# ScalarE's order in the second half of a slot of an expert kernel: rounded rows first, the transposing DMA later

## The chip, the cores and the metric

The kernel runs on one core of a Trainium2 chip. The metric is the time of one execution in device microseconds (us). TensorE (PE) multiplies, VectorE (DVE), ScalarE (ACT) and GpSimd (POOL) work element by element, SyncE (SP) and ScalarE issue DMAs.

## The reference, cut to what matters

An attention with a blocked causal mask is followed by a mixture of eight experts, of which each token uses one. All numbers are float32.

```
q, k, v: (8 batches, 8 heads, 576, 64)
x = softmax(mask(q @ k.T / 8)) @ v          -> 4608 tokens of 512 numbers
expert = argmax(x @ w_gate); gate = softmax weight of that expert
out[token] = gate * (relu(x[token] @ w1[expert]) @ w2[expert])
w1: (8, 512, 1024), w2: (8, 1024, 512)
```

## The kernel before

The first part of the program is the attention with the router. The second part, which begins near 390 us, works on *slots*: 128 tokens that go to the same expert (38 slots in this execution, numbered from 0, each expert's last one filled up). The change touches only this second part. It is written as plain code, in which each engine executes its instructions in the order in which the functions are called, and semaphores (`wait_ge`, `then_inc`) order the engines among each other.

To keep float32 accuracy a factor is split into a rounded part and the rest that the rounding left ("high" and "low"); a product is then made of three rounded products. For one slot `t` the steps are:

- `gather` (POOL) fetches the token rows into `xg`; `rows_in` (PE) transposes them into the PSUM tile `px`.
- `rows_full` (ACT) copies `px` to `xf`, `rows_high` (ACT, line 907) rounds it to `xh`, `rows_pool` (POOL, line 923) makes the rest `xl`.
- `first_half(t, f)` (PE, line 933) makes half `f` of the hidden layer, 512 of its 1024 columns: 8 products that need `xh` and 4 that also need `xl`. It writes the bank `ph` (f = 0) or the bank called `o` in the trace (f = 1). Ahead of half 0 PE's sequencer reads two numbers from memory into registers (lines 965 and 966) and waits for `xh` and `xf`.
- `planes(t, f)` (ACT, line 991) copies that bank into a tile `h` with upper and lower 16 bits apart, `turned(t, f)` (ACT, line 1004) issues a DMA that transposes the tile into `hf` (f = 0) or `turn` (f = 1), `joined(t, f)` (ACT, line 1011) waits for that DMA and puts the 16-bit halves together again, `hidden_high(t, f)` (ACT, line 1020) applies the ReLU and rounds to the high part, `second_relu` (ACT, line 1024) is the ReLU of the unrounded half 1, and `hidden_low(t, f)` (POOL, lines 1051 and 1053) makes the low part. High and low parts both lie in tiles called `low` in the trace.
- `second_pe(t, part)` (PE, line 1083) makes 12 products with half `part`, the last four of which need the low part; `out_act(t)` (ACT, line 1100) scales the result by the gate into `y`, and `out_pool(t)` (POOL, line 1107) writes it out.

DVE meanwhile splits the next expert's weights (lines 1227 and 1233), which SP loads into `raw` (line 1220), as soon as the expert whose place they take is done with.

`period(t)` is one turn of this pipeline. PE's order in it is: half 0 of the first layer of slot t, half 0 of the second layer of slot t-1, the transposes of the rows of slot t+1, half 1 of the first layer of slot t, half 1 of the second layer of slot t-1. ScalarE's order is the order of the calls, and it is what the change alters. `finish` does what is left of the last slot.

Of the kernel before, what the change touches and what calls it, by code (L numbers as in the profile page):

```python
# [792 lines left out]
class Experts:  # L793
# [53 lines left out]
    def run(self):  # L847
# [17 lines left out]
        def gather(t):  # L865
            i = t % 4
            if t < EARLY:
                return
            if t == EARLY:
                pool.wait_ge(sem["ht"], 2)  # L870
                pool.wait_ge(sem["me"], 1)
                pool.wait_ge(sem["st"], 16)
                pool.wait_ge(sem["ga"], 48)
            c = pool.value_load(self.col[t : t + 1, 0:1], min_val=0, max_val=TC - 1)  # L874
            pool.tensor_copy(self.idx[:, t : t + 1], self.stab[:, bass.ds(c, 1)]).then_inc(sem["v1"], 1)  # L875
            pool.wait_ge(sem["v1"], t + 1 - EARLY)
            if t >= 4:
                pool.wait_ge(sem["ya"], t - 3)  # L878
            pool.indirect_dma_start(  # L879
                out=self.xg[i],  # L880
                out_offset=None,
                in_=self.xd[:, :],
                in_offset=bass.IndirectOffsetOnAxis(ap=self.idx[:, t : t + 1], axis=0),
            ).then_inc(sg[i], 16)
# [5 lines left out]
        def rows_in(t):  # L890

            if t >= EARLY:
                pe.wait_ge(sg[t % 4], 16 * gathered(t))
            if t >= 2:
                pe.wait_ge(sem["xa"], 2 * t - 2)
            for k in range(4):
                m = pe.transpose(self.px[:, P * k : P * k + P], self.xg[t % 4][:, P * k : P * k + P], self.ident)
                if t == 1 and k < 2:

                    m.then_inc(sem[("mm1", "mm2")[k]], (3, 1)[k])  # L900
            m.then_inc(sem["xt"], 1)

        def rows_high(t):
            act.wait_ge(sem["xt"], t)
            if t >= 2:
                act.wait_ge(sem["mm1"], 2 * t + 1)
            act.copy(self.xh, self.px).then_inc(sem["xa"], 1)  # L907

        def rows_full(t):
            act.wait_ge(sem["xt"], t)  # L910
            if t >= 2:
                act.wait_ge(sem["xp"], t - 1)
            act.copy(self.xf, self.px).then_inc(sem["xa"], 1)
# [5 lines left out]
        def rows_pool(t):  # L919
            pool.wait_ge(sem["xa"], 2 * t)  # L920
            if t >= 2:
                pool.wait_ge(sem["mm1"], 2 * t + 1)
            pool.tensor_sub(self.xl, self.xf, self.xh).then_inc(sem["xp"], 1)  # L923
# [59 lines left out]
        def planes(t, f):  # L983

            k = 2 * t + f
            act.wait_ge(sem["mm1"], k + 2)
            if k == 4:
                act.wait_ge(sem["ht"], 4)
            elif k >= 7:
                act.wait_ge(sem["hp"], k - 2)  # L990
            act.copy(  # L991
                self.h[k % 3].bitcast(U16).rearrange("p (o c) -> p o c", o=2),
                self.ph[f].bitcast(U16).rearrange("p (c o) -> p o c", o=2),
            ).then_inc(sem["ra"], 1)

        def turned(t, f):

            k = 2 * t + f
            if k == 4:
                act.wait_ge(sem["hp"], 4)  # L1000
            elif k >= 6:
                act.wait_ge(sem["jo"], k - 5)
            act.wait_ge(sem["ra"], k - 1)
            act.dma_start_transpose(
                self.turn[f].bitcast(U16).rearrange("p (k c) -> p k c", c=P), self.h[k % 3].bitcast(U16)
            ).then_inc(st[f], 16)
# [9 lines left out]
        def hidden_high(t, f):  # L1016
            k = 2 * t + f
            act.wait_ge(sem["jo"], k - 3)
            act.wait_ge(sem["mm2"], t)
            act.activation(self.hh[t % 2][:, f], self.h[k % 3], AF.Relu).then_inc(sem["ha"], 2 - f)  # L1020
# [34 lines left out]
        def second_pe(t, part):  # L1055
            e8, off = self.regs[t]
            kinds = ((self.hh, 8192), (self.hl, 8192), (self.hh, 12288))
            if t < 2:
                todo = [(h[t % 2], base, c) for h, base in kinds for c in range(8)]
            else:  # L1060
                todo = [(kinds[i][0][t % 2], kinds[i][1], 4 * f + c) for f in range(2) for i in (0, 2, 1) for c in range(4)]
            if part == 0:
                pe.wait_ge(sem["wh"], e8 + 8 if t >= EARLY else 4)
                if t >= 2:
                    pe.wait_ge(sem["ya"], t - 1)
            if t >= 2:
                pe.wait_ge(sem["ha"], 4 * t + 2 + part)
            elif part == 0:
                pe.wait_ge(sem["ha"], 4 * t + 3)
            for n in range(12 * part, 12 * part + 12):  # L1070
                h, base, c = todo[n]
                if t < 2:
                    if n == 8:
                        pe.wait_ge(sem["hp"], 2 * t + 2)
                    if t == 0 and n >= 16 and c % 2 == 0:
                        pe.wait_ge(sem["wd"], 5 + c // 2)
                    elif n == 16:
                        pe.wait_ge(sem["wd"], e8 + 8)
                elif n == 4:
                    pe.wait_ge(sem["wd"], e8 + 8)  # L1080
                elif n % 12 == 8:
                    pe.wait_ge(sem["hp"], 2 * t + part + 1)
                m = pe.matmul(  # L1083
                    self.py[t % 2],
                    h[:, c // 4, P * (c % 4) : P * (c % 4) + P],
                    wf[:, bass.ds(off + (base + 512 * c), 512)],
                    start=n == 0,
                    stop=n == 23,
                )
            if part == 1:  # L1090
                m.then_inc(sem["mm2"], 1)

        def out_act(t):
            act.wait_ge(sem["mm2"], t + 2)
            if t >= 1:
                act.wait_ge(sy, 16 * t)
            else:

                act.wait_ge(sem["ga"], 48)
            act.activation(self.y, self.py[t % 2], AF.Copy, scale=self.xg[t % 4][:, GATE : GATE + 1]).then_inc(  # L1100
                sem["ya"], 1
            )

        def out_pool(t):
            pool.drain()  # L1105
            pool.wait_ge(sem["ya"], t + 1)
            pool.indirect_dma_start(  # L1107
                out=self.out[:, :],
                out_offset=bass.IndirectOffsetOnAxis(
                    ap=(self.router.first if t < EARLY else self.idx)[:, t : t + 1], axis=0  # L1110
                ),
                in_=self.y,
                in_offset=None,
                bounds_check=self.out.shape[0] - 1,
                oob_is_err=False,
            ).then_inc(sy, 16)
# [21 lines left out]
        def late_half(t):  # L1138
            joined(t, 1)
            hidden_high(t, 1)  # L1140
            second_relu(t)

        def period(t):
            more = t + 1 < NS
            if t == 2:

                for f in range(2):
                    planes(t, f)
                    turned(t, f)
                for f in range(2):  # L1150
                    second_pe(0, f)
                out_act(0)
                out_pool(0)
                gather(4)
                second_pe(1, 0)
                rows_in(3)
                second_pe(1, 1)
                rows_full(3)
                rows_high(3)
                rows_pool(3)  # L1160
                joined(t, 0)
                hidden_high(t, 0)
            else:
                first_half(t, 0)
                planes(t, 0)
                turned(t, 0)
                second_pe(t - 1, 0)
                late_half(t - 1)
                hidden_low(t - 1, 1, pool)
                if more:  # L1170
                    rows_in(t + 1)
                    rows_full(t + 1)
                first_half(t, 1)
                planes(t, 1)
                turned(t, 1)
                if more:
                    rows_high(t + 1)
                    rows_pool(t + 1)
                second_pe(t - 1, 1)
                joined(t, 0)  # L1180
                hidden_high(t, 0)
            out_act(t - 1)
            hidden_low(t, 0, pool)
            out_pool(t - 1)
            if t + 3 < NS:
                gather(t + 3)
# [251 lines left out]
```

## Time and profile before

| | us |
|---|---|
| median of 3 runs (lowest to highest) | 874.76 (873.31 to 879.41) |
| the profiled execution, its own time | 877.96 |
| its span on the core | 876.0 |
| PE busy | 815.2 |
| ACT busy | 597.2 |
| DVE busy | 433.2 |
| POOL busy | 417.7 |

The profiled execution was 3.20 us slower than the median, and 1.96 us of its time lie outside the span. The span falls in two stages: attention and router until some 390 us, the slots after that. In the second stage a period repeats some three dozen times, so a tenth of a microsecond in a period is worth several microseconds in the whole.

### The profile page before, as it was taken

Reading aid. Unit: us, or ns where it says so; the run is one execution under the profiler, and the core shown is the slowest. Engines: PE = TensorE matmul, PEld = TensorE weight load, DVE = VectorE, ACT = ScalarE, POOL = GpSimd, SP = SyncE. Lnnn points to the kernel's source line nnn. Section 1 sums busy time; section 2 is a strip of 40 time slices with the busy share of each in tenths; the row PEclk is TensorE's granted clock in tenths of the full one; section 3 lists DMA queues with packets and bytes.
Section 4 is the critical chain, followed back from the end, with each engine's and each line's share of the span. In section 5 each row is a group of like instructions: output and inputs, shape, how many; then the busy total and the mean of one; then the engine's idle time right before and its main releaser. Section 6 shows DMA issues by size and latency. Waiting matters only on the chain. (4 is left out here: it accounts for less than half of the span.)

```text
span 876.0 us, 16317 instructions
## 1 busy us (share of the span) xinstructions
PE 815.2 (93%) x4982; PEld 614.1 (70%) x4982; DVE 433.2 (49%) x1208; ACT 597.2 (68%) x1254; POOL 417.7 (48%) x428
## 2 busy tenths in 40 slices
PE   5999999999999999998798999999999999999994
PEld 4777767677777777676676777776776777777773
DVE  5778777778787877487017000067367462000000
ACT  6888888888888888444456566655565555656563
POOL 3000223222323422455557656667767666656664
PEclk8999999999999999999999999999999999999997
DMA  5234748363636363528837643468867973434332
GB/s 194 95 116 157 134 134 161 123 151 120 138 125 132 118 133 118 128 60 255 151 91 180 163 97 85 81 173 201 233 174 214 220 187 85 85 73 97 90 79 64
DMA packets 121803, 118.51 MB, mean 135 GB/s; under 512 B 83633, under 2 KB 86961, under 8 KB 121714
## 3 DMA queue, kind: packets, MB, share of 16 engines
q1 hardware_dynamic: 38082, 78.26, 32.1%
q10 hardware_dynamic: 76032, 18.88, 14.0%
q0 software_dynamic: 7600, 20.24, 7.1%
q8 instruction: 49, 0.80, 0.4%
q14 instruction: 40, 0.33, 0.2%
HBM read 77.02 MB, written 21.98 MB: 113 GB/s over the span
## 5 line engine op out<-in xcount | busy, mean ns | idle before, releaser
L1083 PE MATMUL py<-w,low 128*128 (+1 forms) x912 | 232.3, 401 | 14.4 <-POOL low L1053 8.1
L1083 PEld LDWEIGHTS py<-w,low 128*128 128x128 f32 x912 | 171.7, 190 | 62.3 <-POOL low L1053 16.9
L1227 DVE CAST w<-raw 128x1024 fp32r<-128x1024 f32 x60 | 55.6, 967 | 197.9 <-PE o L933 152.6
L247 POOL TENSOR_SCALAR p<-p,rs 128x64 f32<-128x64 f32 x32 | 14.1, 442 | 259.0 <-DVE rs L243 139.8
L1053 POOL TENSOR_TENSOR low<-h,low 128x512 fp32r<-128x512 f32 x72 | 96.9, 1346 | 10.0 <-ACT h L1024 6.7
L933 PE MATMUL ph<-w,xh 128*128 x280 | 73.9, 406 | 22.6 <-ACT xh L907 17.7
L923 POOL TENSOR_TENSOR xl<-xf,xh 128x512 fp32r<-128x512 f32 x38 | 52.8, 1389 | 79.6 <-ACT xh L907 79.5
L1233 DVE TENSOR_TENSOR w<-raw,w 128x1024 fp32r<-128x1024 f32 x60 | 88.8, 1537 | 0.0
L933 PEld LDWEIGHTS ph<-w,xh 128*128 128x128 f32 x280 | 50.8, 189 | 46.1 <-issue 37.7
L1011 ACT COPY h<-turn 128x1024 uint16<-128x1024 uint16 x36 | 42.1, 1169 | 55.6 <-issue 46.1
L933 PE MATMUL o<-w,xh 128*128 x280 | 72.9, 403 | 0.0
L1051 POOL TENSOR_SCALAR h<-h 128x512 f32<-128x512 f32 x36 | 60.9, 1691 | 14.5 <-ACT low L1020 14.4
L1107 POOL DMA_INDIRECT out<-y,idx x35 | 45.7, 1305 | 40.0 <-issue 37.2
L991 ACT COPY h<-ph 128x1024 uint16<-128x1024 uint16 x36 | 36.4, 1012 | 39.5 <-PE ph L933 39.5
L907 ACT CAST xh<-px 128x512 fp32r<-128x512 f32 x38 | 22.3, 586 | 58.5 <-issue 52.5
L991 ACT COPY h<-o 128x1024 uint16<-128x1024 uint16 x36 | 36.4, 1012 | 35.9 <-PE o L933 33.0
L933 PEld LDWEIGHTS o<-w,xh 128*128 128x128 f32 x280 | 50.0, 189 | 8.8
L879 POOL DMA_INDIRECT xg<-xd,idx x38 | 45.4, 1196 | 12.7 <-POOL idx L875 12.7
L234 ACT ACTIVATE pb<-ya,neg 128x320 f32<-128x320 f32 (+2 forms) x93 | 48.5, 532 | 2.5 <-PE pt30x L273 1.8
L234 ACT ACTIVATE pb<-yb,neg 128x320 f32<-128x320 f32 (+2 forms) x93 | 49.4, 546 | 0.0
L731 POOL DMA_INDIRECT tab<-toks,posi x40 | 41.7, 1042 | 15.1 <-issue 14.6
L1020 ACT ACTIVATE low<-h 128x512 fp32r<-128x512 f32 x72 | 45.5, 632 | 4.3 <-issue 0.4
(967 smaller groups left out, 2152.6 us busy)
## 6 DMA issues: line engine op xcount, KB each, us to landing
raw<-w SPq DMA_DIRECT2D x60, 512.0 KB, 5.7
qd<-qT SPq DMA_DIRECT2D x32, 352.0 KB, 3.1
v<-vt SPq DMA_DIRECT2D x32, 352.0 KB, 4.7
kd<-kT SPq DMA_DIRECT2D x32, 288.0 KB, 3.3
xd<-xt SPq DMA_DIRECT2D x7, 1026.0 KB, 12.1
xd<-xg SPq DMA_DIRECT2D x9, 256.5 KB, 6.8
xg<-w SPq DMA_DIRECT2D x8, 256.0 KB, 6.5
xd<-x SPq DMA_DIRECT2D x8, 128.0 KB, 6.6
```

The source lines that it names most:

```text
L234: ins = self.nc.scalar.activation(dst, src, AF.Exp, bias=self.neg[m][:, c : c + 1], scale=1.0, accum_out=self.sums[m][:, c : c + 1])
L879: pool.indirect_dma_start(out=self.xg[i], out_offset=None, in_=self.xd[:, :], in_offset=bass.IndirectOffsetOnAxis(ap=self.idx[:, t : t + 1 ...
L923: pool.tensor_sub(self.xl, self.xf, self.xh).then_inc(sem["xp"], 1)
L933: m = pe.matmul(self.ph[f], x[:, P * k : P * k + P], first_weights(t, k, f, part), start=start and k == 0, stop=stop and k == 3,)
L991: act.copy(self.h[k % 3].bitcast(U16).rearrange("p (o c) -> p o c", o=2), self.ph[f].bitcast(U16).rearrange("p (c o) -> p o c", o=2),).the ...
L1020: act.activation(self.hh[t % 2][:, f], self.h[k % 3], AF.Relu).then_inc(sem["ha"], 2 - f)
L1051: engine.tensor_scalar(hf, hf, 0.0, None, ALU.max).then_inc(sem["rl"], 1)
L1053: engine.tensor_sub(self.hl[t % 2][:, f], hf, self.hh[t % 2][:, f]).then_inc(sem["hp"], 1)
L1083: m = pe.matmul(self.py[t % 2], h[:, c // 4, P * (c % 4) : P * (c % 4) + P], wf[:, bass.ds(off + (base + 512 * c), 512)], start=n == 0, st ...
L1107: pool.indirect_dma_start(out=self.out[:, :], out_offset=bass.IndirectOffsetOnAxis(ap=(self.router.first if t < EARLY else self.idx)[:, t ...
L1227: dve.tensor_copy(hi, raw[m % nr]).then_inc(sem["wh"], 1)
L1233: dve.tensor_sub(lo, raw[m % nr], hi).then_inc(sem["wd"], 1)
```

## The change

In the branch of `period` that all slots from the fourth on take, two ScalarE steps change their places. `rows_high(t + 1)`, the rounding of the next slot's rows, moves from behind `turned(t, 1)` to ahead of `planes(t, 1)`. `turned(t, 1)`, the issue of the transposing DMA of the second half, moves from directly behind `planes(t, 1)` to behind `joined(t, 0)` and `hidden_high(t, 0)`. `rows_pool(t + 1)` moves in the text with `rows_high`, but stands at the same place in POOL's row of instructions. No instruction is added or taken away.

```
                 first_half(t, 1)
-                planes(t, 1)
-                turned(t, 1)
                 if more:
                     rows_high(t + 1)
                     rows_pool(t + 1)
+                planes(t, 1)
                 second_pe(t - 1, 1)
                 joined(t, 0)
                 hidden_high(t, 0)
+                turned(t, 1)
             out_act(t - 1)
```

The built programs differ in ScalarE's row alone; the rows of PE, POOL, DVE and SP are the same. ScalarE, in a period in the middle of the program, from the row copy `xf` (line 913) to the output `y` (line 1100), before:

```order
L913 COPY xf<-px 128x512
L991 COPY h_5888<-o 128x1024
L1004 DMA_TRANSPOSE turn<-h_5888 128x8x128
L907 CAST xh<-px 128x512
L1011 COPY h_5890<-hf 128x1024
L1020 ACTIVATE low_76<-h_5890 128x512
L1100 ACTIVATE y<-py_5897,xg_194 128x512
```

The same stretch of ScalarE after the change:

```order
L913 COPY xf<-px 128x512
L907 CAST xh<-px 128x512
L991 COPY h_5888<-o 128x1024
L1011 COPY h_5890<-hf 128x1024
L1020 ACTIVATE low_76<-h_5890 128x512
L1004 DMA_TRANSPOSE turn<-h_5888 128x8x128
L1100 ACTIVATE y<-py_5897,xg_194 128x512
```

The cast to `xh` moved up past the copy of the planes and the issue of the DMA, and the issue moved down past the joining of the first half and its rounding; the output now stands directly behind the issue.

The first period that is changed is that of slot 3, right behind the specially ordered slot 2. ScalarE there, from its row copy on into slot 4 up to the joining that reads `turn`, before:

```order
L913 COPY xf<-px 128x512
L991 COPY h_5889<-o 128x1024
L1004 DMA_TRANSPOSE turn<-h_5889 128x8x128
L907 CAST xh<-px 128x512
L1011 COPY h_5888<-hf 128x1024
L1020 ACTIVATE low_76<-h_5888 128x512
L1100 ACTIVATE y<-py_5897,xg_194 128x512
L991 COPY h_5890<-ph_5893 128x1024
L1004 DMA_TRANSPOSE hf<-h_5890 128x8x128
L1011 COPY h_5889<-turn 128x1024
```

and after the change:

```order
L913 COPY xf<-px 128x512
L907 CAST xh<-px 128x512
L991 COPY h_5889<-o 128x1024
L1011 COPY h_5888<-hf 128x1024
L1020 ACTIVATE low_76<-h_5888 128x512
L1004 DMA_TRANSPOSE turn<-h_5889 128x8x128
L1100 ACTIVATE y<-py_5897,xg_194 128x512
L991 COPY h_5890<-ph_5893 128x1024
L1004 DMA_TRANSPOSE hf<-h_5890 128x8x128
L1011 COPY h_5889<-turn 128x1024
```

Between the issue of the DMA into `turn` and the joining that reads it there stood six other ScalarE instructions; now there are three.

## Rows read from the trace of the kernel before

**Rows 1.** The page: busy time of PE with its share of the span, and the TensorE clock granted in 40 slices of the span, in tenths.

```profile
PE 815.2 (93%) x4982; PEld 614.1 (70%) x4982; DVE 433.2 (49%) x1208; ACT 597.2 (68%) x1254; POOL 417.7 (48%) x428
PEclk8999999999999999999999999999999999999997
```

**Rows 2.** Groups of instructions by line in the stretch from 435.4 to 845 us, 32 periods: count, busy time and mean of one, then the idle time of the engine just before them and what ended it. The first is the part of `first_half` that needs `xh` (half 0), the second `second_pe`.

```profile
L933 PE MATMUL ph<-w,xh 128*128 x256 | 67.6, 407 | 20.8 <-ACT xh L907 16.4 <-issue 3.7 <-DVE w L1227 0.8
...
L1083 PE MATMUL py<-w,low 128*128 x769 | 194.0, 398 | 6.1 <-POOL low L1053 5.8
```

**Rows 3.** The timeline of one period in which no weights are split: start, duration, engine (ACTq is ScalarE's sequencer, which issues the DMA), line and tiles, and in brackets the idle time before it with what ended it.

```profile
807.83 2.11 PE L933 MATMUL ph<-w,xh 128*128 x8 [0.62 <-ACT xh L907]
...
809.35 1.49 POOL L1051 TENSOR_SCALAR h<-h 128x512 f32<-128x512 f32 x1 [0.50 <-ACT low L1020]
...
810.69 2.96 PE L1083 MATMUL py<-w,low 128*128 x12
810.89 1.01 ACT L991 COPY h<-ph 128x1024 uint16<-128x1024 uint16 x1 [1.05 <-PE ph L933]
810.93 1.30 POOL L1053 TENSOR_TENSOR low<-h,low 128x512 fp32r<-128x512 f32 x1
811.99 1.25 ACTq L1004 DMA_TRANSPOSE hf<-h  x1
...
813.28 1.17 ACT L1011 COPY h<-turn 128x1024 uint16<-128x1024 uint16 x1 [1.38 <-issue]
...
813.49 0.60 PE L897 MATMUL px<-ident,xg 128*128 128x128 f32 x4
...
815.54 0.56 ACT L913 COPY xf<-px 128x512 f32<-128x512 f32 x1
...
816.00 1.30 POOL L1053 TENSOR_TENSOR low<-h,low 128x512 fp32r<-128x512 f32 x1
...
816.68 2.95 PE L1083 MATMUL py<-w,low 128*128 x12
816.87 1.01 ACT L991 COPY h<-o 128x1024 uint16<-128x1024 uint16 x1 [0.77 <-PE o L933]
817.97 1.25 ACTq L1004 DMA_TRANSPOSE turn<-h  x1
819.32 0.58 ACT L907 CAST xh<-px 128x512 fp32r<-128x512 f32 x1 [1.43 <-issue]
819.80 1.17 ACT L1011 COPY h<-hf 128x1024 uint16<-128x1024 uint16 x1
819.98 1.28 POOL L923 TENSOR_TENSOR xl<-xf,xh 128x512 fp32r<-128x512 f32 x1 [2.68 <-ACT xh L907]
820.24 2.11 PE L933 MATMUL ph<-w,xh 128*128 x8 [0.61 <-ACT xh L907]
821.05 0.63 ACT L1020 ACTIVATE low<-h 128x512 fp32r<-128x512 f32 x1
821.59 0.67 ACT L1100 ACTIVATE y<-py,xg 128x512 f32<-128x512 f32 x1
```

**Rows 4.** PE's sequencer (PEldq) between 800 and 830 us: the first register read of line 965 and the wait of line 970; duration min/median/max in ns, first and last start in us.

```profile
L965 PEldq TENSOR_LOAD <-e x2: 303/303/303, 804.8 to 817.4; - x2
...
L970 PEldq EVENT_SEMAPHORE  x2: 51/51/51, 807.6 to 820.0; - x2
```

**Rows 5.** The timeline of one period in which DVE splits weights all the time.

```profile
614.27 1.66 POOL L923 TENSOR_TENSOR xl<-xf,xh 128x512 fp32r<-128x512 f32 x1 [1.47 <-ACT xh L907]
...
614.58 2.09 PE L933 MATMUL ph<-w,xh 128*128 x8 [0.52 <-ACT xh L907]
...
624.92 1.31 POOL L1053 TENSOR_TENSOR low<-h,low 128x512 fp32r<-128x512 f32 x1
...
626.29 1.21 PE L1083 MATMUL py<-w,low 128*128 x4 [0.45 <-POOL low L1053]
...
627.20 1.27 POOL L923 TENSOR_TENSOR xl<-xf,xh 128x512 fp32r<-128x512 f32 x1 [0.97 <-ACT xh L907]
...
627.93 2.11 PE L933 MATMUL ph<-w,xh 128*128 x8 [0.43 <-issue]
```

**Rows 6.** The transposing DMA (line 1004), from issue to landing, first from 640 to 700 us, where weights are loaded, then from 760 to 876 us, where none are.

```profile
DMA to landing us min/median/max: 3.1/4.4/7.9
...
DMA to landing us min/median/max: 3.0/3.1/4.4
```

**Rows 7.** The timeline in slots 3 and 4: the issue for the second half of slot 3, the joining that waits for it, and the products behind that.

```profile
415.62 1.25 ACTq L1004 DMA_TRANSPOSE turn<-h  x1
...
429.12 1.16 ACT L1011 COPY h<-turn 128x1024 uint16<-128x1024 uint16 x1 [6.56 <-DMA turn<-h]
...
431.07 4.54 PE L1083 MATMUL py<-w,low 128*128 x12 [3.57 <-ACT low L1020]
```

**Rows 8.** The starts of half 0 of the first layer (timeline of PE) in slots 4, 5 and 37, between the last two of which lie 32 periods, and the products of the last slot's second layer.

```profile
418.48 2.11 PE L933 MATMUL ph<-w,xh 128*128 x8 [0.47 <-issue]
...
435.41 2.09 PE L933 MATMUL ph<-w,xh 128*128 x8
...
845.06 2.10 PE L933 MATMUL ph<-w,xh 128*128 x8 [0.62 <-ACT xh L907]
...
859.28 6.26 PE L1083 MATMUL py<-w,low 128*128 x20 [2.42 <-ACT low L1020]
```

More of the change, by code (lines that the diff above doesn't have):

```diff
@@ L1173, in period @@
                 first_half(t, 1)
-                planes(t, 1)
-                turned(t, 1)
                 if more:
@@ L1178, in period @@
                     rows_pool(t + 1)
+                planes(t, 1)
                 second_pe(t - 1, 1)
@@ L1181, in period @@
                 hidden_high(t, 0)
+                turned(t, 1)
             out_act(t - 1)
```

## The prediction, as it was put on record

> **What bounds the kernel now.** I read the page first. PE is busy for 93% of the span, no other engine for more than 68%, and the granted clock stands at nine tenths or more in nearly all slices [rows 1]: PE sets the pace, and what can be won is its idle time. The groups by line tell where that lies in the slots. Over the 32 periods from 435.4 to 845 us PE idles 20.8 us ahead of the first products of a slot, of which 16.4 us end with `xh` from line 907, and 6.1 us ahead of products that need a low part from POOL [rows 2]. The rest goes by the timeline.
>
> In a period without weight work [rows 3] one slot starts at 807.83 and the next at 820.24, so it lasts 12.41 us. The reader should follow ScalarE behind the end of half 1. Its copy of the planes starts at 816.87, the DMA issue holds it from 817.97 on, and only at 819.32 does it round `xh`, although the wait of that rounding is for the same event as that of the planes: `rows_high(t+1)` waits for 2t+3 products on `mm1`, and `planes(t,1)` as well. PE has finished its products at 816.68 + 2.95 = 819.63 and starts at 820.24, 0.61 us later, that is 0.34 us behind the end of `xh` (819.32 + 0.58 = 819.90).
>
> **Removed: the wait for `xh`.** After the change `xh` takes the place of the planes: 816.87 to 817.45, some 2 us before PE could use it. What remains is PE's own row of work, counted from start to start in rows 3: half 0 of the first layer 810.69 - 807.83 = 2.86, second layer 813.49 - 810.69 = 2.80, transposes and half 1 816.68 - 813.49 = 3.19, second layer again 2.80 (between two matmul groups that follow without a gap, the tail of one lies under the next). Sum 11.65 us, against 12.41 to 12.46 before: 0.77 us won in each quiet period. The register reads ahead of a slot don't keep PE back there, as they begin at 817.4 and the sequencer then only waits, until 820.0 [rows 4].
>
> **Moved: the issue of the second half's DMA.** ScalarE's steps from 816.87 on become: `xh` 0.48 (819.32 to 819.80, start to start), planes 1.10 (816.87 to 817.97), joining of half 0 1.25 (819.80 to 821.05), so its rounding starts at 819.70, now 1.35 us earlier than before. The issue follows right behind, at about 819.75 instead of 817.97, and keeps ScalarE for 1.35 us. Behind it on ScalarE is the output, at 821.1 instead of 821.59; POOL, which waits for it, gets it no later. Then come the planes of the next slot, which will be wanted at 819.47 + 3.06 = 822.5; the output ends at 821.8. So ScalarE has room. The joining of half 0 is now wanted at 818.45, 6.5 us behind its issue (811.99), where it had 7.8.
>
> Who waits for the moved issue is the joining of half 1 in the next period. That stands 813.28 - 807.83 = 5.45 us behind a slot's start, so at 819.47 + 5.45 = 824.92: 5.2 us from issue to use, where before there were 7.7. In quiet stretches the DMA lands after 3.1 us at the median and 4.4 at most [rows 6], so it costs nothing there. PE itself needs the result at 8.85 us into the slot (816.68), and joining and rounding take 1.8, so the landing may take some 6.7 us before PE waits. Where weights are loaded the median is 4.4 and the worst 7.9 [rows 6]: some landings will be up to 1.2 us late. Nothing in the row excludes that; I put it into the price of the loaded periods.
>
> The Trainium skill bears on this in "DMA: Bandwidth & Descriptors", section "Queues, rings and completion order": each DMA engine takes turns between the queues that have work, packet by packet, so a small transfer pays for a large one beside it. That rule speaks against giving up lead time, the rise from 3.1 to 7.9 us agrees with it, and by it alone the loaded periods would give nothing back, which is the second rival below.
>
> **Sum, quiet periods.** Of the 32 periods between 435.41 and 845.06 [rows 8], 409.65 us together, I count 22 that last 12.40 to 12.64 us. 22 x 0.77 = 16.9 us.
>
> **Sum, loaded periods.** The other ten take 13.25 to 14.53 us, 135.9 together, 13.59 in the mean. DVE is splitting weights there and POOL's steps stretch: `xl` takes 1.66 us where it takes 1.28 in the quiet period [rows 3, 5]. The period from 614.58 to 627.93 shows the chain: POOL ends its low part at 624.92 + 1.31 = 626.23, PE takes its last four products from 626.29 to 627.50 and starts the next slot 0.43 us later, and that gap ends with "issue", not with `xh`, because the sequencer may read its registers only behind the wait for the low part [rows 5]. POOL meanwhile waits 0.97 us for `xh` again. After the change POOL may go straight on: from 614.27 to 626.23 its round takes 11.96 us. Two bounds: if POOL's round hides wholly, a loaded period falls to 11.65 and wins 1.94; if late landings or the low parts take all of it, it wins nothing. I take POOL's round with the 0.43 us gap and 0.1 us of hand-over, 12.49 us, because this row shows both as the next thing late: 1.1 us won, ten times, 11 us.
>
> **Ends.** Behind the last slot PE waits 2.42 us for the rounding of half 0 [rows 8]; that comes 1.35 us earlier, and POOL's and PE's last steps hang on it: -1.3. At the beginning the slots 3 and 4 show the danger once: the DMA issued at 415.62 lands at 429.1, 13.5 us later, and PE stands for 3.57 us [rows 7]. This issue will be 1.75 us later. If the landing is set by the traffic that must drain it doesn't move (0); if it takes as long again, it costs 1.75. Below nothing I don't go, since the DMA can't be earlier. I take the middle, +0.9.
>
> Sum: -16.9 - 11 - 1.3 + 0.9 = -28.3 us. On the profiled execution that is 877.96 - 28.3 = 849.7 us; it was 3.2 us above the median, so 846.5 for the median.
>
> **Rivals.** *Loaded periods hide wholly.* POOL's round (11.96) is only 0.3 us above PE's 11.65, and in a quiet period POOL has slack: it waits 2.68 us for `xh` [rows 3]. If that slack carries over, the ten periods win 19.4 instead of 11: 838. Against it: several loaded periods follow each other, and the register gap stays.
>
> *The second half's DMA takes the place of `xh` in the loaded periods.* Landings of 7 to 8 us against the 6.7 that they may take, each pushing ScalarE's later steps, eat what POOL's round gives: only the quiet periods, the ends and the beginning count, -17.3, or 857.5. For it: the worst landing above. Against it: the periods there stay longer than 11.65, so that the limit is nearer to 7.3.
>
> *The change doesn't do what it says.* If the gap ahead of a slot is PE's register reads, not `xh`, it falls only from 0.62 to the 0.43 or 0.47 that rows 5 and 8 show where `xh` was early: 22 x 0.19 = 4.2 us, and -1.3 and +0.9 at the ends: 870.2. Against it: rows 4, where the reads begin 2.8 us ahead of the slot.
>
> *Slower: the stall of slot 4 in each loaded period.* The issue now stands behind a step that waits for the other half's DMA, so one late landing delays the next issue. The price is known from slot 4: 435.41 - 418.48 = 16.93 us, 4.5 above a quiet period [rows 8]. Ten of these, measured from 13.59, would cost 33, less 17.3: about 890. It decides from landings of some 10.3 us in every loaded period on (the 6.7 that are free, the 1.94 that a loaded period has above the floor, and 1.7 to eat the rest). Outside the beginning the longest in these rows is 7.9.
>
> **How the numbers follow.** Forecast 0.62; loaded periods hidden 0.12; late second half 0.17; register reads 0.05; slower 0.04. The predicted time is that of the first, 846.5. Its own bounds are 841 to 853, from a loaded period's gain of 0.5 to 1.7 us; with the two cases beside it the range is 837 to 861, which leaves out the last two and the far ends of the others. About 1% is what a measurement of this kernel can tell from no change, here 866 to 883.5. The first three cases lie below it (0.91), the fourth within (0.05), the last above (0.04).
>
> **What the changed profile would show.** `xh` directly behind the last product of half 1, and no idle time ended by line 907 ahead of the first layer; quiet periods of 11.65 us (of 12.2 if I am wrong on the register reads); POOL's wait for `xh` shorter, most of it moved behind `xl`, where it waits for the rounding; the DMA into `turn` issued some 2.9 us behind the first ScalarE step that follows half 1 (now `xh`), instead of 1.1; PE's remaining idle time ended by the low part and by "issue". Joinings of `turn` that end a wait for the DMA over 2 us, in more than three or four periods, would make the loaded sum wrong; quiet periods above 12 us would make all of it wrong.

## The result, and the profile after

The changed kernel takes 843.86 us (median of 4 runs, 842.26 to 846.31) against 874.03 us before (4 runs, 872.62 to 879.41): a ratio of 0.966 with a 95% interval of 0.961 to 0.971, 30.2 us less. The forecast was 28.3 us less. The profiled execution took 842.26 us, its span 840.4. Medians and ratios are those of fast runs, which leaves out one run of the kernel with two weight loads in flight, over 1.5% longer than the quickest of that kernel.

The page of the changed kernel, its lines 1, the row of the granted clock, and the two groups of the first and second layer, here from 430.5 to 810.5 us, again 32 periods, which answer to [rows 1, 2]:

```profile
PE 809.2 (96%) x4982; PEld 618.2 (74%) x4982; DVE 421.2 (50%) x1208; ACT 597.6 (71%) x1254; POOL 414.9 (49%) x428
PEclk8999999999999999999999999999999999999998
```
```profile
L1083 PE MATMUL py<-w,low 128*128 x768 | 191.0, 396 | 3.7 <-POOL low L1053 2.5 <-ACT low L1020 1.0
...
L933 PE MATMUL ph<-w,xh 128*128 x256 | 65.2, 397 | 2.8 <-issue 2.7
```

Of the 20.8 us that PE idled ahead of the first products of a slot, 2.8 are left, and 2.7 of these end with "issue", none with `xh`. A quiet period of the changed kernel on the timeline, which answers to [rows 3]:

```profile
773.51 0.59 ACT L907 CAST xh<-px 128x512 fp32r<-128x512 f32 x1 [0.83 <-PE o L933]
773.99 1.02 ACT L991 COPY h<-o 128x1024 uint16<-128x1024 uint16 x1
...
774.89 1.19 ACT L1011 COPY h<-hf 128x1024 uint16<-128x1024 uint16 x1
...
776.04 2.00 PE L933 MATMUL ph<-w,xh 128*128 x8
776.16 0.63 ACT L1020 ACTIVATE low<-h 128x512 fp32r<-128x512 f32 x1
776.24 2.60 ACTq L1004 DMA_TRANSPOSE turn<-h  x1
776.88 1.49 POOL L1051 TENSOR_SCALAR h<-h 128x512 f32<-128x512 f32 x1 [1.41 <-ACT low L1020]
...
778.80 2.94 PE L1083 MATMUL py<-w,low 128*128 x12
778.95 0.69 ACT L1100 ACTIVATE y<-py,xg 128x512 f32<-128x512 f32 x1 [2.16 <-issue]
...
781.58 0.60 PE L897 MATMUL px<-ident,xg 128*128 128x128 f32 x4
...
781.91 1.17 ACT L1011 COPY h<-turn 128x1024 uint16<-128x1024 uint16 x1 [1.38 <-issue]
```

`xh` is done at 774.10 (773.51 + 0.59), PE starts at 776.04 without idle time, and the next slot starts at 787.54: 11.5 us. The slots 10 to 16 and 30 to 36 take 11.51 to 11.54 us each. ScalarE's row is as the order says, the DMA is issued at 776.24, 2.73 us behind the start of `xh`, and is long back when the joining wants it at 781.91. That issue holds ScalarE for 2.60 us, where most take 1.25; even so PE has no gap.

The 32 periods from the start of slot 5 to that of slot 37 (430.55 and 810.59) take 380.0 us, where they took 409.6 [rows 8]. The slots 3 and 4 take 29.2 us instead of 33.4, and what follows the start of slot 37 is 1.1 us shorter. With 0.7 us ahead of slot 3 that makes 35.6 us between the two spans and 35.7 between the profiled times, more than between the medians, since the profiled execution of before lay 3.9 us above its median and that of after 1.6 us below.

### The profile page after: what moved, and what is told of

Read it like the earlier page. It is cut to its first block, busy times and chain, and to the rows that moved or that the text cites. A ratio compares the mean times of both kernels' runs of the same rounds, so it can differ in the third digit from the quotient of the medians.

```text
span 840.4 us, 16317 instructions
## 1 busy us (share of the span) xinstructions
PE 809.2 (96%) x4982; PEld 618.2 (74%) x4982; DVE 421.2 (50%) x1208; ACT 597.6 (71%) x1254; POOL 414.9 (49%) x428
## 3 DMA queue, kind: packets, MB, share of 16 engines
q10 hardware_dynamic: 76032, 18.88, 14.6%
## 5 line engine op out<-in xcount | busy, mean ns | idle before, releaser
L1083 PE MATMUL py<-w,low 128*128 (+1 forms) x912 | 229.8, 400 | 8.1 <-ACT low L1020 5.2
L1011 ACT COPY h<-turn 128x1024 uint16<-128x1024 uint16 x36 | 42.0, 1168 | 55.9 <-issue 33.4
L1233 DVE TENSOR_TENSOR w<-raw,w 128x1024 fp32r<-128x1024 f32 x60 | 78.5, 1365 | 0.0
L1051 POOL TENSOR_SCALAR h<-h 128x512 f32<-128x512 f32 x36 | 57.4, 1593 | 42.1 <-ACT low L1020 42.1
L933 PE MATMUL ph<-w,xh 128*128 x280 | 71.4, 397 | 4.0 <-issue 3.1
L1100 ACT ACTIVATE y<-py,xg 128x512 f32<-128x512 f32 x38 | 26.2, 689 | 44.3 <-issue 30.1
L731 POOL DMA_INDIRECT tab<-toks,posi x40 | 41.6, 1041 | 15.1 <-issue 14.9
L339 PE MATMUL o<-fold,oT 128*128 128x144 f32 x256 | 45.4, 300 | 0.9 <-ACT oT L311 0.6
```

The costliest lines, as they stand in the source:

```text
L339: mm(t[:, i], self.oT[m, 0][:, o : o + P], w, start=True, stop=True)
L933: m = pe.matmul(self.ph[f], x[:, P * k : P * k + P], first_weights(t, k, f, part), start=start and k == 0, stop=stop and k == 3,)
L1051: engine.tensor_scalar(hf, hf, 0.0, None, ALU.max).then_inc(sem["rl"], 1)
L1083: m = pe.matmul(self.py[t % 2], h[:, c // 4, P * (c % 4) : P * (c % 4) + P], wf[:, bass.ds(off + (base + 512 * c), 512)], start=n == 0, st ...
L1233: dve.tensor_sub(lo, raw[m % nr], hi).then_inc(sem["wd"], 1)
```

## Experiments

The theory behind the result: PE's start behind `xh` cost what the prediction said; the order gives two things, `xh` early and the rounding of half 0 early; and the long periods that are left come from transposing DMAs that land late beside the weight loads. The rivals: the early `xh` is all; or POOL, slowed beside VectorE's splitting, makes them long.

**The rows alone.**

```
                 first_half(t, 1)
                 if more:
                     rows_high(t + 1)
                     rows_pool(t + 1)
                 planes(t, 1)
+                turned(t, 1)
                 second_pe(t - 1, 1)
                 joined(t, 0)
                 hidden_high(t, 0)
-                turned(t, 1)
```

> The changed kernel with the issue of the second half's DMA put back directly behind the planes: only the rounding of the rows has moved, ahead of planes and issue. If the wait for xh were all that the change removed, this runs as the changed kernel does, 844 us, with quiet periods of 11.5 us, or better, since the second half's DMA has its old lead. If the move of the issue is needed as well, because it lets joining and rounding of half 0 come 1.35 us earlier: the rounding of half 0 then comes 1.65 us behind a slot's start instead of 0.12, POOL's low part is ready near 5.3 us, PE wants it at 4.6 us, and a quiet period takes about 12.2 us with some 0.66 us of idle time that ends with POOL's low part: about 864 us in all.

Measured: 866.17 us (862.62 to 870.75) against 876.51 for the kernel before beside it, a ratio of 0.990 (0.984 to 0.996). Quiet periods take 12.23 to 12.28 us. One of them on the timeline, and below it the sum of that wait:

```profile
781.04 0.59 ACT L907 CAST xh<-px 128x512 fp32r<-128x512 f32 x1 [1.36 <-PE o L933]
...
783.57 2.00 PE L933 MATMUL ph<-w,xh 128*128 x8
...
785.16 0.63 ACT L1020 ACTIVATE low<-h 128x512 fp32r<-128x512 f32 x1
...
787.46 1.31 POOL L1053 TENSOR_TENSOR low<-h,low 128x512 fp32r<-128x512 f32 x1
...
788.82 1.20 PE L1083 MATMUL py<-w,low 128*128 x4 [0.47 <-POOL low L1053]
```
```profile
PE py L1083 <- POOL low L1053: 16.5, 29, 1.5
```

PE starts the slot without a wait and stands five microseconds later, for the low part of half 0, because its rounding waits behind the DMA issue: the wait for `xh` has become a wait for POOL. Of the 0.9 us that the whole change wins in a quiet period this part alone wins less than 0.2, as the second case of the expectation says.

**The issue alone.**

```
                 first_half(t, 1)
+                planes(t, 1)
                 if more:
                     rows_high(t + 1)
                     rows_pool(t + 1)
-                planes(t, 1)
                 second_pe(t - 1, 1)
```

> The changed kernel with the rounding of the rows put back behind the planes: only the issue of the second half's DMA has moved, behind joining and rounding of half 0. xh then starts 1.0 us later than in the changed kernel, still some 0.8 us ahead of the end of PE's products, and everything behind it stands where the changed kernel has it: quiet periods of 11.5 us, 844 us. If it matters that xh is rounded first (because POOL's xl, 1.0 us later, delays its round), quiet periods stay at 11.5 us, but loaded ones grow by up to 1 us: 850 to 854 us.

Measured: 843.47 us (842.16 to 849.77), 0.965 (0.960 to 0.971) of the kernel before, quiet periods of 11.51 to 11.54 us: the same as the changed kernel. That `rows_high` stands ahead of `planes` gives nothing that these runs can tell; what counts is that the issue has left the place ahead of both roundings.

**One weight load in flight.** SP waits for the load before it:

```
                     if m >= nr:
                         sp.wait_ge(sem["wd"], m - nr + 5)
+                    if m >= 5:
+                        sp.wait_ge(sraw[(m - 1) % nr], 16 * loads_so_far_of_that_buffer)
                     load(m, row)
```

(`loads_so_far_of_that_buffer` stands for a count that the code works out.)

> The changed kernel, but SP issues a weight load only when the one before it has landed, so that one of 512 KB is in flight instead of up to four. If the long periods that are left (13 to 14.6 us) come from transposing DMAs that land late beside the weight loads, the landings stay below about 5 us, these four periods come down by some 7 us together, and the time is about 837 us, unless PE now waits for weights. If they come from POOL being slowed while DVE splits weights, nothing changes: 844 us.

Measured: 839.92 us (838.27 to 843.48), 0.961 (0.956 to 0.965) of the kernel before, an interval that overlaps with the changed kernel's. The 32 periods stay at 380.3 us together, but not the same ones are long. Of the four that the expectation speaks of, slots 17, 22 and 25 come down from 41.6 us together to 35.6, close to three quiet periods (34.6). Slot 27 stays at 13.4, and slot 24 rises from 11.6 to 15.9, because PE waits for weights there, 4.2 us in all, 2.6 of them in slot 24:

```profile
PE py L1083 <- DVE w L1233: 4.2, 2, 2.6
```

The 4 us in the time come from the slots 3 and 4 (25.4 us instead of 29.2). So the first expectation held in part, with its "unless". That quicker landings did it isn't shown: this profile has no landing times of the transposing DMA, and loads that come one by one also spread VectorE's splitting, which waits for each of them.

**The issue still later**, behind the next slot's planes:

```
                 planes(t, 0)
+                if t > 3:
+                    turned(t - 1, 1)
                 turned(t, 0)
...
                 joined(t, 0)
                 hidden_high(t, 0)
-                turned(t, 1)
```

(`finish` issues the last slot's.)

> The changed kernel with the second half's DMA issued still later, behind the planes of the next slot's half 0: some 3.9 us behind the slot's start instead of 0.2. By the working of the lead (landing after 3.1 us, joining and rounding 1.8 us, PE wants it at 8.7 us into the slot) the limit is just passed in quiet periods: 12.0 to 12.4 us each, with PE waiting for ScalarE's rounding and POOL's low part of half 1, 860 to 872 us in all. If the lead were of no account, 11.5 us and 844 us.

Measured: 864.13 us, one run. Quiet periods are mostly 11.75 to 11.87 us, a little better than I had worked out, while most of those with weight work take 12.6 to 14.7. The joining now nearly always waits for the DMA:

```profile
ACT h L1011 <- DMA turn<-h: 99.4, 35, 4.9
```

The lead has a price, then: 0.3 us in a quiet period and much more beside loads. The waits of PE that I expected aren't what the quiet periods lose: from 739 to 836 us PE waits once for the rounding (0.9 us), 1.8 us in all end with "issue", and none with POOL's low part. Places between this one and that of the changed kernel were not tried.

**Two weight loads in flight.**

```
+                    if m >= 6:
+                        sp.wait_ge(sraw[(m - 2) % nr], 16 * loads_so_far_of_that_buffer)
```

> The changed kernel with at most two weight loads in flight, where the run with one showed quicker starts of slots 4 and 5 but a wait of PE for weights in slot 24. If late landings beside the loads make the periods that are left long, and one load in flight was only too few for VectorE, the wait for weights goes and the time is 835 to 838 us. If the number of loads in flight matters only in the slots 3 and 4, the 32 periods behind them stay at 380 us together and the time is 840 us; if it doesn't matter at all, 844.

Measured: 846.70 us (median of three, 841.59 to 852.07; the fourth took 855.13), 0.964 (0.957 to 0.971) of the kernel before: not better than the changed kernel, and its runs lie wider apart. In the profiled one, 852.07 us and so the longest of the three, the 32 periods took 391.0 and the longest landing that the trace has from 563 to 712 us was 12.5. My expectation failed: how late a transposing DMA lands is not simply a matter of how many loads are in flight.

**One weight load in flight in the kernel before.** The edit is that of the run with one load, made in the kernel before.

> The kernel before the change, with one weight load in flight. If its ten loaded periods were long because POOL is slowed while VectorE splits weights and because each slot starts behind xh, while the lead of 7.7 us covered the late landings, they stay at 13 to 14 us and only the stall of slot 4 (4.5 us) goes: about 1% faster than before, not more. If landings beside the loads made them long in that kernel too, they fall towards 12.5 us: 2% faster than before, some 858 us.

Measured: 872.7 us (870.02 to 877.15, 10 runs) against 876.48 (13 runs), 0.996 (0.994 to 0.999). That is 0.4% less, where the first theory gave about 1%. Its loaded periods stay long (32 periods: 413.7 us), and the slots 3 and 4 take 27.3 us instead of 33.4, as that theory says. The run doesn't rule the second one out, since the landings got no shorter: the longest from 563 to 712 us is 11.2 us, against 7.9 and 9.0 in the two profiles of the kernel before.

**Both kernels a second time**, without an edit.

> The changed kernel once more, for a second profile: quiet periods of 11.5 us again. If the short slot 4 (12.8 us against 16.9 before the change) belongs to the change, it is below 14 us again; if it was the luck of one execution, it may be 15 to 17.

> The kernel before the change once more, for a second profile: quiet periods of 12.4 us again. If the stall of slot 4 (16.9 us) belongs to the kernel before, it is there again; if it was the luck of one execution, slot 4 takes 13 to 15 us, as in the run in which only the rows were moved (14.1).

Measured: 843.34 and 877.11 us. The stall of slot 4 belongs to the kernel before. Its second profile, ScalarE and PE in slots 3 and 4:

```profile
416.20 1.25 ACTq L1004 DMA_TRANSPOSE turn<-h  x1
...
429.49 1.16 ACT L1011 COPY h<-turn 128x1024 uint16<-128x1024 uint16 x1 [6.17 <-DMA turn<-h]
431.45 4.41 PE L1083 MATMUL py<-w,low 128*128 x12 [3.19 <-ACT low L1020]
```

The second profile of the changed kernel:

```profile
418.45 1.25 ACTq L1004 DMA_TRANSPOSE turn<-h  x1
...
423.81 1.16 ACT L1011 COPY h<-turn 128x1024 uint16<-128x1024 uint16 x1 [1.38 <-DMA turn<-h]
```

Issued 2.25 us later, it is back 5.7 us earlier. Slot 4 takes 11.63 us in the changed kernel (12.78 in its first profile), 16.40 in the one before.

**Half of each load, and little splitting, in either kernel.** Four runs are to part the two causes of long periods. The loads:

```
-                sp.dma_start(dst, self.chunk(row, c))...
+                src = self.chunk(row, c)
+                half = (lambda x: x[:, 0:512]) if c < 4 else (lambda x: x[:, 0])
+                sp.dma_start(half(dst), half(src))...
```

and the splitting (`...` stands for the rest of a line):

```
-                dve.tensor_sub(lo, raw[m % nr], hi)...
+                n = 1024 if e < 3 else 64
+                dve.tensor_sub(lo[:, 0:n], raw[m % nr][:, 0:n], hi[:, 0:n])...
```

> The changed kernel, which loads only half of each weight block of the experts 1 to 7 (the other half keeps what lay there, so the products of these experts are not the reference's); VectorE's work and all orders stay. If the long periods come from transposing DMAs that share the DMA engines with the loads, landings stay under 6 us and the 32 periods come from 380 to about 371 us, 11.6 each: 832 us. If they come from POOL being slowed beside VectorE's splitting, they stay at 380: 843 us.

> The changed kernel, in which VectorE makes the low parts of the weights of the experts 3 to 7 for 64 of 1024 columns only (the rest keeps older low parts, so these products are not the reference's): some 1.4 us less of VectorE per block beside POOL, the same loads, issued somewhat earlier. If the late DMAs make the long periods, those of the slots 16 to 27 stay (12 periods of some 149 us together in two profiles) or get worse, as the loads come in a tighter burst; if POOL's slower steps make them, they fall to 11.6 each, 139 us together.

> The kernel before, with half of each weight block of the experts 1 to 7 left out of the loads. If its loaded periods were long because of POOL (the working of the prediction), they stay at 13 to 14 us, 408 us for the 32 periods, and only slot 4's stall goes. If the landings made them long there too, the 32 periods come to about 400 us.

> The kernel before, with low parts for only 64 of 1024 columns of the weights of the experts 3 to 7. If POOL beside VectorE made the loaded periods long, those of the slots 16 to 27 fall to 12.4 to 12.6 us, 150 us for the twelve instead of 159; if the landings did, they stay.

Measured were 841.16, 859.39, 873.6 and 867.7 us, one run each, beside 870.18 for the kernel before. Other runs of that kernel lie between 872 and 880, so single times tell little here, and the argument goes by the stretches of the profiles. The twelve slots 16 to 27, in which most of the weight work lies, from the start of slot 16 to that of slot 28 on PE's timeline:

| kernel | start of slot 16 | of slot 28 | difference, us | longest landing from 563 to 712 us |
|---|---|---|---|---|
| before | 574.30 | 733.26 | 159.0 | 7.9 |
| before, second profile | 574.88 | 732.27 | 157.4 | 9.0 |
| before, half loads | 570.06 | 728.32 | 158.3 | 5.4 |
| before, little splitting | 571.98 | 723.95 | 152.0 | 9.1 |
| after | 558.37 | 706.67 | 148.3 | 9.0 |
| after, second profile | 559.68 | 708.43 | 148.8 | 9.8 |
| after, half loads | 559.37 | 705.04 | 145.7 | 5.7 |
| after, little splitting | 562.61 | 724.63 | 162.0 | 14.7 |

In the kernel before, quicker landings change nothing, and less work of VectorE takes some 6 us away although the longest landing is no shorter. POOL's steps are shorter with it; the first of them in the kernel before from 563 to 712 us, and below it the same with little splitting:

```profile
L1051 POOL TENSOR_SCALAR h<-h 128x512 f32<-128x512 f32 x12 | 22.8, 1900 | 3.7 <-ACT low L1020 3.6
```
```profile
L1051 POOL TENSOR_SCALAR h<-h 128x512 f32<-128x512 f32 x11 | 17.2, 1565 | 6.1 <-ACT low L1020 6.1
```

So POOL beside VectorE's splitting accounts for most of what the loaded periods of that kernel take above a quiet one: at 12.42 us each the twelve slots would take 149.0, and 7 of the 10 us above that go (5 of 8 by the second profile). In the changed kernel landings count too. Less splitting makes it 14 us slower; its loads are issued 0.6 us apart instead of 1.1 or more, and landings take up to 14.7 us. The worst place, in slots 21 and 22 of that run:

```profile
643.99 1.25 ACTq L1004 DMA_TRANSPOSE turn<-h  x1
...
658.08 1.16 ACT L1011 COPY h<-turn 128x1024 uint16<-128x1024 uint16 x1 [11.16 <-DMA turn<-h]
...
660.05 4.47 PE L1083 MATMUL py<-w,low 128*128 x12 [8.12 <-ACT low L1020]
```

Half the loads make it faster by about 3 us, in one profile, which leaves some long periods. One of them, slot 17 of that run, which takes 13.0 us:

```profile
580.97 1.31 POOL L1053 TENSOR_TENSOR low<-h,low 128x512 fp32r<-128x512 f32 x1
...
582.33 1.19 PE L1083 MATMUL py<-w,low 128*128 x4 [0.44 <-POOL low L1053]
...
583.94 2.11 PE L933 MATMUL ph<-w,xh 128*128 x8 [0.42 <-issue]
```

That is POOL's round with the register reads behind it. At 11.53 us each the twelve slots would take 138.4: of the 10 us above that in the changed kernel about 3 go with half of the loads, and about 7 stay. A run that takes VectorE's work away without moving the loads is missing, so the share of POOL in these 7 is read from slots such as this one and not measured. The 371 us that I expected for the 32 periods, if landings were all, did not come (378.3).

## Why the prediction was right

The terms of the sum, in us won (the first two add up to the 32 periods; the ten loaded slots are those named below, in both pairs):

| term | forecast | first pair of profiles | second pair |
|---|---|---|---|
| 22 quiet periods | 16.9 | 17.8 | 18.8 |
| ten loaded periods | 11 | 11.8 | 7.5 |
| behind the start of the last slot | 1.3 | 1.1 | 1.9 |
| slots 3 and 4 | -0.9 | 4.1 | 5.7 |

**The wait for `xh`** went as forecast, and quiet periods won a little more than forecast: from 12.42 to 11.53, 0.89 us instead of 0.77. (Slot 25, quiet before, became long, so the 22 won less than 22 times that.) The floor of 11.65 was too high because its first term, 2.86 us for half 0 of the first layer, was read behind a gap. Without the gap the same step takes 778.80 - 776.04 = 2.76. The rival of the register reads fell in quiet periods: there is no gap at all.

**The moved issue** cost nothing in quiet periods, as worked out. But the prediction put the whole gain under the wait for `xh` and mentioned only in passing that the rounding of half 0 comes 1.35 us earlier. The run with the rows alone shows that this is half of the bargain: without it most of the gain turns into a wait for POOL's low part. The run with the issue alone shows that the cause is the issue's place: moved by itself it gives both, `xh` in time and the early rounding. The sign that the prediction named, more than three or four joinings of `turn` that wait over 2 us for the DMA, was just kept: three in the first profile, four in the second.

**Loaded periods.** The ten that were loaded before (slots 7, 8, 16, 17, 19, 21, 22, 23, 26, 27) took 135.9 us together and now take 124.1: 1.18 us each against 1.1 forecast. The size was right in this pair, the picture half so. I had expected ten periods near 12.5 us, bound by POOL's round and the register gap. Seven of them lie at 11.5 to 12.0, as in the first rival, with POOL's round hidden, and slots 17, 22 and 27 at 14.6, 13.9 and 13.2, with slot 25 (13.1) beside them. The seven won 1.66 us each, slots 17, 22 and 27 nearly nothing (0.2 together): that this adds up to about ten times 1.1 is luck. In the second profile the longest are slots 8, 17, 20, 22 and 24 (12.5 to 15.3), and the ten won 7.5 us. What is late in slot 17 is the rounding of half 0, and behind it POOL:

```profile
571.40 1.17 ACT L1011 COPY h<-hf 128x1024 uint16<-128x1024 uint16 x1 [2.54 <-DMA hf<-h]
...
572.73 1.25 ACTq L1004 DMA_TRANSPOSE turn<-h  x1
...
573.53 2.12 PE L1083 MATMUL py<-w,low 128*128 x8 [0.64 <-ACT low L1020]
...
576.59 1.21 PE L1083 MATMUL py<-w,low 128*128 x4 [0.94 <-POOL low L1053]
```

Here the DMA of the *first* half came late, which I had given 6.5 us without a second thought, and the issue of the second half stood behind its joining, just as the rival that ends slower has it, only in few slots instead of ten. Slot 25 waits for the DMA of the second half, 3.38 us ahead of its joining at 676.06, and slot 27 for no late DMA at all: PE waits 0.46 us for POOL's low part there and 0.42 us behind it. Of the rivals that named a mechanism, the late landing was thus at work, partly in the other DMA, and POOL's round as forecast in a few slots.

**The ends.** The last slot won 1.1 us (1.3 forecast). The beginning is the term with the wrong sign: +0.9 forecast, and the slots 3 and 4 became 4.1 us shorter in the first pair of profiles and 5.7 in the second. The step that failed reads "Below nothing I don't go, since the DMA can't be earlier". The DMA was issued later and landed earlier, in both profiles. That the loads make the landing late there is borne out by the kernel before with half of the loads: no transposing DMA takes more than 4.8 us from 412 to 428 us, and slot 4 takes 12.41 us instead of 16.9. Its slot 3 grows, though, from 16.4 to 18.6, as PE waits 4.4 us for POOL's `xl` there, so that both slots together win only 2.4. Why an issue 1.7 to 2.25 us later escapes the loads was not tried by itself. The loads around it gain as well: the slowest of them took 11.0 and 11.1 us to land in the two profiles of before, 5.9 and 7.0 in the changed kernel. In the changed kernel's first profile:

```profile
417.35 1.25 ACTq L1004 DMA_TRANSPOSE turn<-h  x1
...
425.12 1.16 ACT L1011 COPY h<-turn 128x1024 uint16<-128x1024 uint16 x1 [3.27 <-DMA turn<-h]
427.09 3.06 PE L1083 MATMUL py<-w,low 128*128 x12 [0.30 <-ACT low L1020]
```

**Turns between queues.** The section of the Trainium skill that I weighed ("DMA: Bandwidth & Descriptors", "Queues, rings and completion order") says that each DMA engine takes turns, packet by packet, between the queues that have work for it; that a small transfer pays for a large one beside it was my conclusion. The runs with half of the loads agree as to the direction: the longest landing falls from 9.0 or 9.8 to 5.7 us. What I made of it for the sum, no gain in loaded periods, was wrong by 12 us in the first pair and 7.5 in the second, since in most of them the landing still came within the lead. Nor is the transposing DMA small in the time that it takes of the engines. From 412 to 432 us in the kernel before (queue, packets, MB, share of the 16 engines' time), two transposing DMAs, q10, take as much as four weight loads, q1:

```profile
q10 hardware_dynamic: 2112, 0.52, 43.7%
q1 hardware_dynamic: 576, 2.10, 40.8%
```

## What to carry to other kernels

An instruction that only issues a DMA still holds its engine's row (here 1.25 us and more); ask what stands behind it, and let those steps go ahead whose results the bounding engine wants soonest, as long as the DMA's lead stays above its landing time. When a wait is taken away by reordering, work out the next deadline of each step that is in the same row: moving the rows alone won a fifth of what the whole change did in a quiet period, and moving the issue alone won all of it. An ample lead can hide late transfers; after it has been spent, transfers that used to cost nothing can cost something (here some 3 of the 10 us that the slots 16 to 27 take above the floor).

## What the runs showed of the hardware

Where no weights were loaded, a transposing DMA took 3.1 us from issue to landing at the median (3.0 to 4.4) [rows 6]; beside weight loads it took up to 13.5 us (slot 3 of the kernel before [rows 7]), and up to 14.7 where the loads were issued 0.6 us apart. With half of each load the longest was 5.7 us from 563 to 712 us. Issuing one 2.25 us later brought it back 5.7 us sooner, in the slots where four loads are issued at about the same time. Fewer loads in flight didn't make landings shorter: the longest from 563 to 712 us was 11.2 us with one load at a time in the kernel before (7.9 and 9.0 without that limit), and 12.5 with two in the changed kernel (9.0 and 9.8 without). What decides how late a landing is remains open. POOL's step of line 1051 took 1.90 us in the mean beside VectorE's splitting and 1.57 with little of it.
